# Windowed attention, a gated MLP and a channel mix: attention weights unfolded, values multiplied by whole and half key tiles

## The chip, the cores and the metric

The kernel runs on one core of a Trainium2 chip. The metric is the device time of one execution in microseconds (us). Three runs of the kernel before took 586.86 to 588.02 us, median 587.9. One further execution was profiled: 587.97 us by the same clock, with a span of 586.3 us from the first to the last traced instruction. The engines are PE (TensorE: matmuls; PEld is its weight load), DVE (VectorE), ACT (ScalarE), POOL (GpSimd) and SP, which issues all DMAs.

## The reference

Three layers follow each other; batch is 4, the sequence 576, the model width 512.

```python
# 1. attention: 8 heads of 64, a causal window of 128, ALiBi bias
scores = 0.125 * q @ k.T                                   # rel = query - key
scores = where((rel >= 0) & (rel < 128), scores - slope_h * |rel|, -1e9)
attn = exp(scores - max); attn /= sum(attn) + 1e-9
x = concat_heads(attn @ v)                                 # (4, 576, 512)
# 2. gated MLP with mixing over the sequence
h = gelu_tanh(x @ w_in); u, v = h[..., :512], h[..., 512:]
v_n = layernorm(v) * g_ln
v_s = w_sg @ v_n (over the sequence) + b_sg
x = x + (u * v_s) @ w_out
# 3. channel mix with a token shift
xk = mu_k*x + (1-mu_k)*x_prev; xr = mu_r*x + (1-mu_r)*x_prev
out = sigmoid(xr @ w_r) * (relu(xk @ w_k)**2 @ w_v)
```

Rows of the window matter below. Cut the sequence in 9 blocks of 64. A query block n sees key block n in its lower triangle, n-1 wholly, and n-2 in its strict upper triangle.

## The kernel before

**Recording and planning.** Helpers of `Build` record every operation with its cost in the author's model, with the engines that may do it (`"dp"`: DVE or POOL, `"ad"`: ACT or DVE, `"adp"`: all three) and with its reads and writes. `Rec.schedule` then picks an engine and an order for all of them by due times, shifted by the tables `PRI` and `ENG`. It also puts filler matmuls on `tri` (`filler`, names `wps`) where PE would idle. What comes out is one fixed order for each engine.

**Attention** works on 16 pairs of heads (two heads share the 128 partitions; four pairs make a batch). For each query block n of a pair, `s_item` makes scores of 64 queries against up to 192 keys on 64x64 quarters of the array, two heads at once. `s_tile` adds the mask and takes the maximum (DVE, L811), then exponentiates with row sums (ACT, L494). The exponentials p are 192 wide: key blocks n-2, n-1 and n. As n-2 holds a strict upper and n a lower triangle, L817 adds the one onto the other (the fold, `p<-p` 128x64), which leaves 128 columns. `t_step` and `t4_step` transpose these 9 blocks of a pair on PE (`tf<-ident,p`, 4, 4 and 1), copy them out of PSUM to `pf`, and split the fold again: `keep` makes an upper and a lower copy with a triangular select on POOL (L534) or a product with the mask `tri` on DVE (L541). `av_items` multiplies by the values (`a<-pf,rawv`): all 128 keys of a tile, two heads side by side on 128x64 halves of the array, 14 matmuls of 128 columns and 4 of 64. The first four pairs scale by the reciprocal row sum afterwards (`rt`, L879); the others scale p itself (L764). From pair 5 on (`MERGE`) the values' matmuls of pair c-1 and the first scores of pair c are one PE step (`av_s`).

**The MLP** of a batch (`moe1`) uses float32 split in a high and a low fp32r part (`xg`, `vhl`, `gg`, `w_in_t`, ...) and three products a group. `merge` interleaves the steps of batch b with the attention of batch b+1. Its PE groups are named `d`: `d<-w_in_t,xg` (v tiles, 512 columns), `d<-xg,w_in_t` (u tiles, 288), `d<-w_sg_t,vhl`, `d<-gg,w_out_t`. Weights arrive as 64-bit floats and are decoded on ACT and DVE (`wdec`) before the split.

**The channel mix** (`phase2`) runs last over chunks of 512 tokens: `d<-xk,wk`, then `rps<-w_r_t,xr`, then `vps<-w_v_t,k2h` and `k2l`.

**SBUF** is dealt out pool by pool in the order of `base`. With the sizes in the code, the pool `wp` begins at a multiple of 512 bytes. `xp` behind it has two buffers of 4x577 floats, each rounded up to 9,248 bytes, so that the tiles of the next pool `gp` (`xg`, `vhl`, `gg`, `k2h`, `k2l`) begin 64 bytes past a multiple of 512; `wk`, in another pool, begins 64 bytes short of one, and so do `xk`'s tiles.

Of the kernel before, what the change touches and what calls it, by code (L numbers as in the profile page):

```python
# [42 lines left out]
    ("rawv0", "sp"): -26306, ("rel", "pool"): 2432, ("rin", "dve"): 123164, ("rin.0", "dve"): 49476, ("rin.1", "dve"): 20510, ("rl", "act"): 67514,  # L43
# [4 lines left out]
    ("v.1", "dve"): -54577, ("v.1", "dve/pool"): 8029, ("vhl", "act/dve/pool"): -30835, ("vhl", "dve"): 107701, ("vhl", "dve/pool"): 115592,  # L48
    ("vhl.1", "act/dve/pool"): -138686, ("vhl.1", "dve"): -100786, ("vhl.1", "dve/pool"): 207877, ("vps", "pe"): -69329, ("vsg", "dve"): -48464,
    ("vsg", "dve/pool"): -215093, ("vsg.1", "dve"): 18451, ("vsg.1", "dve/pool"): 63786, ("w_in_t.0", "act/dve/pool"): 159389,  # L50
    ("w_in_t.0", "dve/pool"): -93050, ("w_out_t.1", "act/dve/pool"): -59118, ("w_out_t.1", "dve/pool"): -286676, ("w_r_t", "act/dve/pool"): -119201,
    ("w_r_t", "dve/pool"): 111587, ("w_sg_t.1", "act/dve/pool"): 278977, ("w_sg_t.1", "dve/pool"): -19852, ("w_v_t", "act/dve/pool"): -29476,
    ("w_v_t", "dve/pool"): 8489, ("wdec", "act"): 69975, ("wdec", "dve"): 110168, ("wdec.0", "act"): 285, ("wdec.0", "dve"): 657275,
# [562 lines left out]
def attn_gmlp_rwkv_kernel(  # L616
# [108 lines left out]
    def width(n):  # L725
        return 64 * min(n + 1, 3)
# [614 lines left out]
```

## Time and profile before

| | before |
|---|---|
| median of 3 runs | 587.9 us |
| the profiled execution | 587.97 us |
| its span | 586.3 us |
| PE busy | 573.0 us (98%) |
| DVE busy | 415.0 us (71%) |
| ACT busy | 289.7 us (49%) |
| POOL busy | 176.9 us (30%) |
| instructions | 11,019 |

Busy time counts an engine as occupied from the start of an instruction to its end; matmuls overlap each other, and fillers count as busy PE, so PE near 100% does not mean that all of it is wanted work. The 1.7 us between span and time lie around the traced instructions.

### The profile page before, as it was taken

Reading aid. Unit: us, or ns where it says so; the run is one execution under the profiler, and the core shown is the slowest. Engines: PE = TensorE matmul, PEld = TensorE weight load, DVE = VectorE, ACT = ScalarE, POOL = GpSimd, SP = SyncE. Lnnn points to the kernel's source line nnn. Section 1 sums busy time; section 2 is a strip of 40 time slices with the busy share of each in tenths; the row PEclk is TensorE's granted clock in tenths of the full one; section 3 lists DMA queues with packets and bytes.
Section 4 is the critical chain, followed back from the end, with each engine's and each line's share of the span. In section 5 each row is a group of like instructions: output and inputs, shape, how many; then the busy total and the mean of one; then the engine's idle time right before and its main releaser. Section 6 shows DMA issues by size and latency. Waiting matters only on the chain.

```text
span 586.3 us, 11019 instructions
## 1 busy us (share of the span) xinstructions
PE 573.0 (98%) x4050; PEld 486.0 (83%) x4050; DVE 415.0 (71%) x1174; ACT 289.7 (49%) x778; POOL 176.9 (30%) x321
## 2 busy tenths in 40 slices
PE   7898999999999999999999999999999999999997
PEld 4575789997899978999799987888888888888885
DVE  6999899876878768876899999962924463616032
ACT  4776787755665546762664377430503340413041
POOL 4534684753735527234355002300100000000000
PEclk9799999999999999999999999999999999999999
DMA  8765533324021220002713175331000100000000
GB/s 280 197 165 155 137 99 97 77 66 145 23 64 42 64 104 22 3 2 83 268 55 109 45 232 169 106 106 55 18 37 20 53 1 37 18 19 36 19 19 36
DMA packets 22998, 48.13 MB, mean 82 GB/s; under 512 B 4384, under 2 KB 12832, under 8 KB 22432
## 3 DMA queue, kind: packets, MB, share of 16 engines
q1 hardware_dynamic: 22944, 47.42, 26.6%
q8 instruction: 32, 0.52, 0.4%
q14 instruction: 22, 0.18, 0.1%
HBM read 37.97 MB, written 9.45 MB: 81 GB/s over the span
## 4 chain that ended last, share of the span: by engine, by line
PE 85%; DVE 10%; ACT 1%; issue 1%; POOL 1%; DMA 1%; SPq 0%; POOLq 0%; DVEq 0%; ACTq 0%
PE d L472 50%; PE vps L472 17%; PE rps L472 8%; PE s L472 4%; PE a L472 4%; PE tf L480 2%; DVE p L811 2%; DVE wdec L551 1%; DMA wraw<-in_w_sgT_dram 1%; DVE wdec L568 1%; DVE gt L551 1%; DVE p L514 0%; DVE v L551 0%; DVE w_sg_t L514 0%; DVE bn L998 0%
## 5 line engine op out<-in xcount | busy, mean ns | idle before, releaser
L472 PE MATMUL d<-xk,wk 128*128 128x512 f32 (+1 forms) x480 | 102.9, 368 | 0.0
L472 PEld LDWEIGHTS d<-xk,wk 128*128 128x128 f32 x480 | 84.4, 188 | 15.8
L472 PE MATMUL vps<-w_v_t,k2h 128*128 128x512 f32 x288 | 93.7, 396 | 0.0
L494 ACT ACTIVATE p<-p,nmax 128x192 f32<-128x192 f32 (+2 forms) x144 | 61.5, 429 | 30.0 <-DVE nmax L811 29.6
L472 PE MATMUL d<-w_in_t,xg 128*128 128x512 f32 (+1 forms) x240 | 63.1, 410 | 2.0 <-DVE xg L504 1.5
L472 PEld LDWEIGHTS vps<-w_v_t,k2h 128*128 128x128 f32 x288 | 54.1, 188 | 12.9
L472 PE MATMUL d<-w_sg_t,vhl 128*128 128x288 f32 x448 | 63.8, 298 | 0.0
L472 PEld LDWEIGHTS d<-w_sg_t,vhl 128*128 128x128 f32 x448 | 60.3, 188 | 1.7 <-issue 0.8
L472 PE MATMUL vps<-w_v_t,k2l 128*128 128x512 f32 x144 | 57.0, 396 | 0.0
L472 PEld LDWEIGHTS d<-w_in_t,xg 128*128 128x128 f32 (+1 forms) x240 | 42.3, 183 | 16.6 <-DVE xg L504 2.0
L472 PE MATMUL d<-xg,w_in_t 128*128 128x288 f32 x384 | 55.3, 299 | 0.3 <-ACT x L502 0.3
L472 PE MATMUL d<-gg,w_out_t 128*128 128x288 f32 x384 | 54.9, 297 | 0.0
L534 POOL TENSOR_SCALAR_AFFINE_SELECT pf<-pf 128x512 f32<-128x512 f32 (+2 forms) x70 | 43.4, 636 | 37.2 <-ACT pf L502 20.7
L472 PEld LDWEIGHTS d<-xg,w_in_t 128*128 128x128 f32 x384 | 52.0, 189 | 3.1 <-issue 1.1
L472 PE MATMUL rps<-w_r_t,xr 128*128 128x512 f32 x216 | 53.1, 392 | 0.3 <-ACT r L494 0.3
L472 PEld LDWEIGHTS d<-gg,w_out_t 128*128 128x128 f32 x384 | 51.9, 188 | 1.7 <-issue 1.4
L514 DVE TENSOR_TENSOR r<-vps,r 128x512 f32<-128x512 f32 x18 | 12.3, 687 | 54.5 <-ACT r L494 28.1
L472 PEld LDWEIGHTS rps<-w_r_t,xr 128*128 128x128 f32 x216 | 40.1, 188 | 9.2 <-ACT r L494 0.7
L811 DVE CUSTOM_DVE_ANT_0 p<-s,mask 128x192 f32<-128x192 f32 (+1 forms) x144 | 41.2, 328 | 8.1 <-PE s L472 8.1
L506 POOL TENSOR_SCALAR xk<-mt 128x64 fp32r<-128x64 f32 (+4 forms) x9 | 6.9, 766 | 130.6 <-DVE mt L551 129.3
L494 ACT ACTIVATE rl<-d 128x512 f32<-128x512 f32 (+1 forms) x40 | 21.7, 555 | 46.2 <-PE d L472 41.7
L494 ACT ACTIVATE r<-rps 128x512 f32<-128x512 f32 x18 | 10.7, 599 | 66.3 <-PE rps L472 66.2
(123 smaller groups left out, 996.0 us busy)
## 6 DMA issues: line engine op xcount, KB each, us to landing
rawqk<-in_qk_dram SPq DMA_DIRECT2D x32, 288.0 KB, 4.5
rawv<-in_v_dram SPq DMA_DIRECT2D x32, 160.0 KB, 2.3
xs<-x SPq DMA_DIRECT2D x4, 1154.0 KB, 4.7
out_dram<-r SPq DMA_DIRECT2D x18, 256.0 KB, 2.0
st<-in_w_in_dram SPq DMA_DIRECT2D x8, 512.0 KB, 7.3
wraw<-in_w_k_dram SPq DMA_DIRECT2D x8, 512.0 KB, 4.6
wraw<-in_w_v_dram SPq DMA_DIRECT2D x8, 512.0 KB, 3.7
wraw<-in_w_out_dram SPq DMA_DIRECT2D x8, 256.0 KB, 2.6
```

Source lines behind the costliest of these rows:

```text
L472: pe.matmul(real(o), real(l), real(r), start=st, stop=sp, **ex)
L480: pe.transpose(real(o), real(i), real(d))
L494: nc.scalar.activation(real(out), real(in_), func, scale=scale, **kw)
L506: alts.append(("pool", 148 + 0.83 * in_.n, lambda: nc.gpsimd.tensor_scalar(real(out), real(in_), 1.0, 0.0, ALU.mult, ALU.add)))
L514: alts.append(("dve", self._dve(out.n, False), lambda: nc.vector.tensor_tensor(real(out), real(a), real(b), op)))
L534: nc.gpsimd.affine_select(out=real(out), in_=real(in_), pattern=pat, compare_op=cmp, fill=0.0, base=0, channel_multiplier=-sgn)
L551: alts.append(("dve", cost or self._dve(out.n, False, isinstance(s, Vw)), lambda: nc.vector.scalar_tensor_tensor(real(out), real(a), real( ...
L568: alts.append(("dve", self._dve(out.n, fast and not a.ps, ptr), lambda: nc.vector.tensor_scalar(real(out), real(a), real(s1), real(s2), op ...
L811: K.raw("dve", 70 + w / 0.96, lambda: nc.vector.tensor_tensor_reduce(out=real(po), in0=real(s), in1=real(ma), scale=-0.125, scalar=3.0e38, ...
```

## The change

1. For the first 8 pairs (`UNF`), p is neither folded nor masked. Two neighbouring query blocks share a tile p of 384 columns, and `t_step` transposes 13 blocks of 128x128 (4, 4, 4, 1) where there were 9. The later pairs fold, transpose 9 and mask as before, with one select for each kind of triangle.
2. For all pairs, `av_items` multiplies each whole key tile t with the two query blocks that see all of it (2t+1, 2t+2) on 128x64 halves, and the half tiles with the one query block each that sees 64 of its keys, on 64x64 quarters. The upper halves of a tile go to a second PSUM tile `e`, which is added to x afterwards: one more DVE operation a pair, two in the first four pairs.
3. `tri` has 20 blocks and is made by 6 selects on POOL and 2 copies on DVE.
4. In `base`, `xp` goes behind `gp` and `up`, so that `xg`, `vhl`, `gg`, `k2h` and `k2l` begin at multiples of 512 bytes.
5. The cost of float32 matmuls in the planner's model is new, and `PRI` and `ENG` have other numbers throughout.

```diff
-    ("a", "pe"): -69879, ("a.0", "pe"): 271509, ("a.1", "pe"): 145744, ("bn", "dve"): -21776, ...
+    ("a", "pe"): 374006, ("a.0", "pe"): 37152, ("a.1", "pe"): -13497, ("bn", "dve"): 212851, ...
...
+UNF = 8
+KEEP = ((0, 0), (1, 1), (0, 0), (1, 1), (0, 0), (0, 1), (1, 0), (0, 1), (1, 0), (0, 1))
...
-          "attc": 1, "raw": 3, "wraw": 2, "v": 4, "sp": 20, "pt": 2,
+          "attc": 1, "raw": 3, "wraw": 2, "v": 4, "sp": 10, "pt": 2,
-    base = ("const", "wp", "xp", "gp", "up", "tp", "st", "dr", "psD", "psS", "psT")
+    base = ("const", "wp", "gp", "up", "xp", "tp", "st", "dr", "psD", "psS", "psT")
...
     def s_tile(c, n, bank):
-        p = T("sp", [P, 192], F32, "p")
+        if n % 2 == 0:
+            PP[c] = T("sp", [P, 384], F32, "p")
+        p = PP[c]
...
+        f = po
+        if c >= UNF:
+            f = 320 if n % 2 else 0
+            if n > 1:
+                K.tt(p[:, f:f + 64], p[:, o:o + 64], p[:, o + 128:o + 192], ALU.add, "dp")
+            k = 128 if n == 0 else o + 64 * (n % 2)
+            f = p[:, k:k + 128]
+            PW[c].append(f)
+        elif n % 2 or n == 8:
+            PW[c] += [p[:, k:k + P] for k in ((128, 256) if n == 1 else (0, 128) if n == 8 else (0, 128, 256))]
+        PT[c, n] = f
+
+    def t_steps(c):
+        return ((0, 4), (4, 8), (8, 9)) if c >= UNF else ((0, 4), (4, 8), (8, 12), (12, 13))
...
+        if c >= UNF:
+            z = max(b, 2)
+            K.keep(pf[:, 14 + 2 * z:14 + 2 * e, :], pf[:, 2 * z:2 * e, :], 0)
+            K.keep(v, v, 6 if b else 4)
...
         for t in range(4):
             for j in range(2):
-                its.append((a[64 * j:64 * j + 64, 2 * t:2 * t + 2, :], rv[j][:, t, :], pair(4 * t, j), t == 0, t == 3, SG))
-            if t < 3:
-                for j in range(2):
-                    its.append((a[64 * j:64 * j + 64, 2 * t + 2:2 * t + 4, :], rv[j][:, t, :], pair(18 + 4 * t, j), False, False, SG))
-        for k, i in ((3, 30), (4, 16)):
+                r, w = slice(64 * j, 64 * j + 64), (6 if un else 4) * t + 3 - j
+                if t < 3:
+                    its.append((a[r, 2 * t + 1:2 * t + 3, :], rv[j][:, t, :], pf[:, w:w + 2 + 2 * j:1 + 2 * j, :], t == 0, False, SG))
+                else:
+                    its.append((a[r, 7, :], rv[j][:, t, :], pf[:, w, :], False, False, SG))
+                    its.append((e[r, 0, :], rv[j][:, t, :], pf[:, w + 1 + 2 * j, :], True, False, SG))
+        for j in range(2):
+            r = slice(64 * j, 64 * j + 64)
+            its.append((e[r, 0, :], rv[j][:, 4, :], pf[:, (24 if un else 30) + j, :], False, False, SG))
+        for i in range(4):
+            lo, up = (6 * i, 6 * i) if un else (14 + 4 * i if i else 0, 16 + 4 * i)
             for j in range(2):
-                its.append((a4b[64 * j:64 * j + 64], rv[j][:, k, :], pf[:, i + j, :], k == 3, k == 4, SG))
-        return a, a4b, its
+                its.append((a[64 * j:64 * j + 64, 2 * i, :], rv[j][0:64, i, :], pf[0:64, lo + j, :], False, i == 3, SG))
+            for j in range(2):
+                if i:
+                    its.append((e[64 * j:64 * j + 64, i, :], rv[j][64:P, i - 1, :], pf[64:P, up + 1 - j, :], False, i == 3, SG))
+        return a, e, its
...
+        x = x_t[b]
+        xo, odd = x[:, ch, 129:513].split(P)[:, :, 64:P], e[:, 1:4, :]
         if c < RROW:
-            K.tt(x_t[b][:, ch, 1:513], a.flat(), rt, ALU.mult)
+            K.tt(x[:, ch, 1:513], a.flat(), rt, ALU.mult)
+            ro = rt[:, 128:512].split(P)[:, :, 64:P]
+            K.tt(ro, odd, ro, ALU.mult)
+            odd = ro
         else:
-            K.copy(x_t[b][:, ch, 1:513], a.flat())
-        K.copy(x_t[b][:, ch, 513:577], a4b)
+            K.copy(x[:, ch, 1:513], a.flat())
+        K.tt(xo, xo, odd, ALU.add, "dp" if c < RROW else "d")
+        K.copy(x[:, ch, 513:577], e[:, 0, :])
...
+    for x in sorted(set(KEEP)):
+        for k in (k for k in range(len(KEEP)) if KEEP[k] == x and k not in (2, 3, 8, 9)):
+            v = K.tri[:, 2 * k:2 * k + 2].two()
+            K.raw("pool", 240, lambda v=v, f=K.select(v, *x): f(real(v), real(v)), [v], [v])
+    for k in (2, 8):
+        K.copy(K.tri[:, 2 * k:2 * k + 4].flat(), K.tri[:, 2 * k - 4:2 * k].flat(), "d")
```

On PE, the values' matmuls of pair 1 before (`a` and the numbered `a` are its two PSUM tiles, the second for the last query block), with the scores and transposes behind them:

```order
L472 MATMUL a<-pf,rawv 64x128 x14
L472 MATMUL a_585<-pf,rawv 64x64 x4
L472 MATMUL s<-rawqk 64x192 x2
L480 MATMUL tf<-ident,p 128x128 x8
L472 MATMUL s<-rawqk 64x64 x2
```

The same place after (`a_540` is the tile `e` of the code):

```order
L488 MATMUL a<-pf,rawv 64x128 x6
L488 MATMUL a<-pf,rawv 64x64
L488 MATMUL a_540<-pf,rawv 64x64
L488 MATMUL a<-pf,rawv 64x64
L488 MATMUL a_540<-pf,rawv 64x64 x3
L488 MATMUL a<-pf,rawv 64x64 x4
L488 MATMUL a_540<-pf,rawv 64x64 x2
L488 MATMUL a<-pf,rawv 64x64 x2
L488 MATMUL a_540<-pf,rawv 64x64 x2
L488 MATMUL a<-pf,rawv 64x64 x2
L488 MATMUL a_540<-pf,rawv 64x64 x2
L488 MATMUL s<-rawqk 64x192 x2
```

Fourteen wide matmuls have become six; the last 14 narrow ones are the quarters, `a` from the lower 64 keys and `a_540` from the upper 64.

On DVE, between the masked scores of pairs 1 and 2, before (`st_405` is staged `w_in`):

```order
L514 TENSOR_TENSOR p<-p 128x64
L504 COPY pf<-tf_530 128x128
L514 TENSOR_TENSOR p<-p 128x64
L541 TENSOR_TENSOR pf<-pf,tri 128x128
L568 TENSOR_SCALAR wdec<-wdec 128x512
L541 TENSOR_TENSOR pf<-pf,tri 128x128
L514 TENSOR_TENSOR p<-p 128x64 x2
L551 SCALAR_TENSOR_TENSOR wdec<-st_405,wdec 128x512
```

The same place after:

```order
L596 TENSOR_SCALAR wdec<-wdec 128x512
L579 SCALAR_TENSOR_TENSOR wdec<-st_408,wdec 128x512
L520 COPY rt<-rt 128x512
L596 TENSOR_SCALAR wdec<-wdec 128x512
L530 TENSOR_TENSOR w_in_t<-wdec,w_in_t 128x512
L530 TENSOR_TENSOR x<-a,rt 128x512
...
L530 TENSOR_TENSOR rt<-a_540,rt 128x3x64
L579 SCALAR_TENSOR_TENSOR wdec<-st_408,wdec 128x512
L530 TENSOR_TENSOR x<-x,rt 128x3x64
```

Folds and mask products are gone from the row; the two operations on the second PSUM tile have come in.

On POOL, from the making of `tri` on, before:

```order
L1199 MEMSET tri 128x1024
L877 MEMSET x 128x4
L534 AFFINE_SELECT tri<-tri 128x512 x2
L516 TENSOR_TENSOR p<-p 128x64 x3
L534 AFFINE_SELECT pf<-pf 128x512
L820 MEMSET p 128x64
L571 TENSOR_SCALAR p<-p,rin 128x128
```

After:

```order
L1245 MEMSET tri 128x1280
L546 AFFINE_SELECT tri<-tri 128x128 x6
L848 MEMSET p 128x64 x2
L522 TENSOR_SCALAR w_in_t<-wdec 128x512
L848 MEMSET p 128x64 x2
L522 TENSOR_SCALAR w_in_t<-wdec 128x512
```

POOL has lost folds and selects here and takes part of the split of `w_in`.

## Rows read from the trace of the kernel before

**Rows 1.** The page: an engine's busy time; the granted clock in 40 slices, tenths.

```profile
PE 573.0 (98%) x4050; PEld 486.0 (83%) x4050; DVE 415.0 (71%) x1174; ACT 289.7 (49%) x778; POOL 176.9 (30%) x321
...
PEclk9799999999999999999999999999999999999999
```

**Rows 2.** Stretches of the span: their length, each engine's busy time (instructions), clock, DMA.

```profile
10.00:92.00 82.00, 75.92 (x806) 57.35 (x804) 76.62 (x278) 62.47 (x206) 42.88 (x83) 0.94 0.60 161
92.00:280.00 188.00, 188.00 (x1723) 171.17 (x1724) 146.46 (x465) 110.94 (x344) 93.75 (x170) 1.00 0.21 62
280.00:360.00 80.00, 79.98 (x477) 71.75 (x475) 75.70 (x147) 47.66 (x87) 24.27 (x34) 1.00 0.44 149
360.00:587.00 227.00, 222.19 (x1008) 182.70 (x1008) 111.01 (x268) 65.68 (x135) 10.58 (x14) 1.00 0.12 40
```

**Rows 3.** PE in order of time: start, length, instructions merged [idle time before, its releaser].

```profile
22.82 0.33 PE L472 MATMUL s<-rawqk 64*64 64x64 f32 x4 [1.66 <-ACT x L502]
...
56.45 0.50 PE L472 MATMUL d<-w_in_t,xg 128*128 128x512 f32 x1 [1.46 <-DVE xg L504]
```

**Rows 4.** The chain of waits from 0 to 110 us: start, length, what it passes through.

```profile
17.39 0.44 DVE pf L541
...
19.04 0.67 DVE w_in_t L514
19.71 0.41 DVE p L514 x3
...
23.87 1.33 PE s L472 x12
...
40.70 0.36 DVE p L811
...
54.42 0.74 DVE w_sg_t L514 x2
...
90.77 0.78 DVE p L568 x4
```

**Rows 5.** DVE and POOL groups up to 92 us: count, busy time, mean ns, idle before.

```profile
L514 DVE TENSOR_TENSOR p<-p 128x64 f32<-128x64 f32 x30 | 7.1, 255 | 0.7 <-ACT p L494 0.7
L541 DVE TENSOR_TENSOR pf<-pf,tri 128x128 f32<-128x128 f32 x7 | 2.7, 383 | 0.0
...
L534 POOL TENSOR_SCALAR_AFFINE_SELECT pf<-pf 128x512 f32<-128x512 f32 x18 | 13.9, 779 | 6.0 <-DVE pf L541 3.8 <-ACT pf L502 1.7
L516 POOL TENSOR_TENSOR p<-p 128x64 f32<-128x64 f32 x19 | 7.6, 409 | 6.8 <-ACT p L494 6.4
```

**Rows 6.** PE in order of time: values, then scores; the x12 are its end.

```profile
153.13 1.98 PE L472 MATMUL a<-pf,rawv 128*64 128x128 f32 x36
...
154.49 0.62 PE L472 MATMUL a<-pf,rawv 128*64 128x128 f32 x12
155.04 0.77 PE L472 MATMUL s<-rawqk 64*64 64x64 f32 x16
```

**Rows 7.** PE in batch 1's v tiles, in order of time.

```profile
138.41 7.26 PE L472 MATMUL d<-w_in_t,xg 128*128 128x512 f32 x30
145.51 1.04 PE L480 MATMUL tf<-ident,p 128*128 128x128 f32 x8
146.31 1.65 PE L472 MATMUL d<-w_in_t,xg 128*128 128x512 f32 x6
```

**Rows 8.** The chain of waits from 340 us on.

```profile
371.59 6.82 PE d L472 x30
...
394.94 14.01 PE vps L472 x60
...
425.68 2.75 PE rps L472 x12
```

**Rows 9.** The start, in order of time: POOL's `tri`, DVE's first masked score.

```profile
5.18 1.35 POOL L534 TENSOR_SCALAR_AFFINE_SELECT tri<-tri 128x512 bf16<-128x512 bf16 x2
...
7.41 0.23 DVE L811 CUSTOM_DVE_ANT_0 p<-s,mask 128x64 f32<-128x64 f32 x1 [0.61 <-PE s L472]
```

More of the change, by code (lines that the diff above doesn't have):

```diff
@@ L48 @@
[L48 to L51, printed above, removed]
@@ new lines @@
+    ("rawv0", "sp"): -136893, ("rel", "pool"): 41476, ("rin", "dve"): 34972, ("rin.0", "dve"): -509504, ("rin.1", "dve"): 1422,
[3 rows of a table added]
+    ("tri", "dve"): -22967, ("tri", "pool"): 133552, ("u", "dve"): -55884, ("u.1", "dve"): 217151, ("v", "dve"): -90958, ("v", "dve/pool"): 707269,
+    ("v.1", "dve"): -119475, ("v.1", "dve/pool"): 106315, ("vhl", "act/dve/pool"): 56077, ("vhl", "dve"): -212679, ("vhl", "dve/pool"): -383927,
+    ("vhl.1", "act/dve/pool"): 53485, ("vhl.1", "dve"): 21972, ("vhl.1", "dve/pool"): -79968, ("vps", "pe"): 142878, ("vsg", "dve"): 40,
@@ L175, in real @@
                 a = a.bitcast(x)
+            elif k == "sp":
+                a = a.rearrange("p (a b) -> p a b", b=x)
+            elif k == "two":
+                a = a.rearrange("p (s h) q -> p s h q", h=2)
             elif k == "bro":
@@ L461, in mm @@
     def mm(self, items, **kw):
-        cost = 0.0
-        for o, l, r, *_ in items:
-            cost += 14.0 if o.box()[0] >= 64 and o.ids.shape[0] <= 64 or l.ids.shape[0] == 64 <= l.box()[0] else (4 * r.n / 2.4 + 10) if l.dtype == F32 else (r.n / (1.2 if l.dtype == BF16 else 2.4) + (20 if l.base.name in ("k2h", "k2l") else 14))
-        if items[0][1].dtype == F32 and (items[0][1].ids.shape[0] == 64 or items[0][1].ids.shape[1] == 64):
-            cost += 320.0
+        tiled = [(i[1].ids.shape[0] <= 64, i[1].ids.shape[1] <= 64) for i in items]
+        if items[0][1].dtype == F32 and any(map(any, tiled)):
+            free, t = {}, 0.0
+            for (o, l, r, *_), (rt, ct) in zip(items, tiled):
+                at = [(a, c) for a in ((l.box()[0] // 64,) if rt else (0, 1)) for c in ((o.box()[0] // 64,) if ct else (0, 1))]
+                t = max([t] + [free.get(x, 0.0) for x in at])
+                for x in at:
+                    free[x] = t + 4 * r.n / 2.4
+            cost = max(free.values()) + 255 + 215 * sum(x != y for x, y in zip(tiled, tiled[1:]))
+        else:
+            cost = sum(r.n / (1.2 if l.dtype == BF16 else 2.4) + 14.0 for _, l, r, *_ in items)
         pe = self.nc.tensor
@@ L524, in square, with select, go, keep @@
             ("pool", 140 + 2.12 * x.n, lambda: nc.gpsimd.tensor_tensor(real(x), real(x), real(x), ALU.mult))], [x, x], [x])
-    def keep(self, out, in_, upper, engs="p"):
-        nc = self.nc
-        m = in_.ids.shape[1]
-        sgn, cmp = (-1, ALU.is_gt) if upper else (1, ALU.is_ge)
-        pat = [[0, m // 4], [64 * sgn, 2], [0, 2], [sgn, 64]] if m % 4 == 0 else [[0, 2], [sgn, 64]]
+    def select(self, v, upper, odd):
+        sgn, cmp = (-1, ALU.is_gt) if upper else (1, ALU.is_ge)
+        def go(out, in_):
+            self.nc.gpsimd.affine_select(out=out, in_=in_, pattern=[[0, v.ids.shape[1]], [0, 2], [sgn, 64]],
+                                         compare_op=cmp, fill=0.0, base=64 * sgn * odd, channel_multiplier=-sgn)
+        return go
+    def keep(self, out, in_, k0, engs="dp"):
+        nc = self.nc
+        m = in_.ids.shape[1] // 2
+        kinds = KEEP[k0:k0 + m]
+        parts = []
+        for x in sorted(set(kinds)):
+            ks = [k for k in range(m) if kinds[k] == x]
+            vo, vi = (z.two()[:, ks[0]:ks[-1] + 1:2 if len(ks) > 1 else 1] for z in (out, in_))
+            parts.append((self.select(vo, *x), vo, vi))
+        t = self.tri[:, 2 * k0:2 * (k0 + m), :]
         def go():
-            nc.gpsimd.affine_select(out=real(out), in_=real(in_), pattern=pat,
-                                    compare_op=cmp, fill=0.0, base=0, channel_multiplier=-sgn)
+            for f, vo, vi in parts:
+                f(real(vo), real(vi))
         alts = []
-        if "p" in engs and not in_.ps:
-            alts.append(("pool", 147 + 0.715 * out.n, go))
-        t = self.tri[:, int(upper), :m, :]
+        if "p" in engs:
+            alts.append(("pool", 147 * len(parts) + 0.715 * out.n, go, len(parts)))
         if "d" in engs:
             alts.append(("dve", self._dve(out.n, False), lambda: nc.vector.tensor_tensor(real(out), real(in_), real(t), ALU.mult)))
-        return self.r.op(alts, [in_] + ([t] if "d" in engs else []), [out])
+        return self.r.op(alts, [in_, t], [out])
     def sub(self, out, a, hi, engs="dp"):
@@ L847, in av_items @@
         a = T("psD", [P, 8, 64], F32, "d", "a") if c >= NC else T("psT", [P, 8, 64], F32, "t", "a")
-        a4b = T(pool, [P, 2, 256], F32, "s" if pool == "psS" else "t", "a4")[:, 0, 0:64]
+        e = T(pool, [P, 2, 256], F32, "s" if pool == "psS" else "t", "a4").flat()[:, 0:256].split(64)
         pf, its = PTc.pop(c), []
         rv = [rawv.pop(2 * c + j) for j in range(2)]
-        def pair(i, j):
-            lo, hi = i + j, i + 3 - j
-            return pf[:, min(lo, hi):max(lo, hi) + 1:abs(hi - lo), :]
+        un = c < UNF
@@ L914, in trans @@
         def trans():
-            for b in range(2):
-                add(480, t_step, prev, b)
-            add(120, t4_step, prev)
+            for b, e in t_steps(prev):
+                add(120 * (e - b), t_step, prev, b, e)
         def tail():
```

152 lines of the change are left out of this document (71 added, 81 removed), and 43 rows, old and new, of the table PRI.

## The prediction

> **What bounds the kernel now.** I read the busy times first: PE 98%, DVE 71%, ACT 49%, POOL 30% [rows 1]. That says PE, but busy PE includes fillers, so the stretches come next [rows 2]. From 92 us to the end PE is busy without a break, and DVE has room in most of it (146.5 of 188 us from 92 to 280); only from 280 to 360 is DVE nearly full too (75.7 of 80). Before 92 us it is the other way round: DVE is busy 76.6 of 82 us, and PE waits for x and its split ("ACT x", "DVE xg") [rows 3]. The chain of waits agrees: it runs over DVE's short operations from about 7 to 24 us, over PE from 23.87 to 40.70, and over DVE again from there to 92 [rows 4]. So there are two stages with two prices. Up to 92 us (the front) an instruction is worth what it takes DVE, about 68 of those 85 us. After that only PE's time counts.
>
> **The front: DVE's list.** I counted the two orders up to the first `vsg`, which is the first result of batch 0's third product; both versions have by then done the values of pairs 0 to 5, so the lists compare. DVE issues 311 instructions before and 272 after.
>
> Gone are 30 folds: three in a row take 0.41 us on the chain, 0.137 each [rows 4], 4.1 us. (Their busy time, 7.1 us for the 30 [rows 5], counts overlap with the neighbours, so I take steps along the chain throughout.) Gone are 10 mask products, 7 of 128 columns and 3 of 256; the one shown took 0.44 us on the chain and the 7 were busy 2.7 us, 0.38 each [rows 4, 5]; at 0.30 to 0.40 each, 3.4 us. 11 scalings of p at 0.78/4 = 0.195 make 2.1 [rows 4]. Seven splits of `w_sg` go to POOL at 0.74/2 = 0.37 [rows 4], 2.6. Ten copies and scalings of 288 to 576 columns go to POOL or ACT; I put them at the price of such a split, some 0.4 each, 4.0. Sum 16.2.
>
> New are four splits of `vhl` and one of `xg`, at 0.67 at most like that of `w_in_t` [rows 4], 3.1; four casts of `w_in_t`, a third product's width at under that price, say 0.35, 1.4; ten operations of 128x192 on the second PSUM tile, whose form is not in the trace: between the fold's 0.137 (64 columns) and 0.37 (288), by width 0.27, 2.7 (bounds 1.4 to 3.7); three scalings of 192 columns, 0.25 each, 0.8; two copies of `tri`, 0.2 to 0.5 each, 0.6; five others, 1.5. Sum 10.1. Net 6.1 us less on DVE, with 4.5 to 7.5 as bounds from those of the parts.
>
> Does another engine take over? POOL loses 24 selects of the two kinds and 19 folds, over 21 us of its 43 [rows 2, 5], and gets seven splits and some casts: no. ACT gets 16 scalings of 192 columns for 14 of 128, six copies out of PSUM (13 transposed blocks a pair, not 9) and loses six casts of `w_in_t`: about 3.5 us on 62.5 of 82 [rows 2]. It stays under DVE's share, but not by much. PE gets four more transposes a pair and has fillers to give up. So of the 6.1 us, the share that lies on DVE's part of the chain is gained: 68/85, 4.9 us.
>
> At the very start something is lost. The first masked score on DVE starts at 7.41 us, 0.9 us after POOL's selects of `tri`, which take 1.35 us [rows 9]. Now six selects on POOL make `tri`, and two copies on DVE, which wait for the selects, stand in DVE's queue ahead of the first masked score; everything on DVE waits behind them. At 0.3 us each the selects end about 0.7 us later, the copies add 0.6, and the 0.9 us in between absorb most: 0.3 us lost (0 to 1.2). Front: -4.6 us (range 0 to -8; below nothing too if PE's clock, 0.94 over the front and 7 tenths in the second slice [rows 1, 2], is granted in full).
>
> **After 92 us: the values on PE.** In units of 128 columns and one of float32's two passes, a pair takes 16 units before (14 wide matmuls are 7 side by side, 2 passes each; 4 narrow ones make 2). The x36 rows start at 153.13 and the last x12 at 154.49: 12 units in 1.36 us, 0.113 each; the remaining 4 units take 0.45 of the 0.55 us up to the scores, which leaves 0.10 for the change from halves to quarters [rows 6]. After: three wide pairs 6 units, the narrow ones on halves 3, the quarters 4 rounds of 64 columns, 4 units if all four quarters work at once. 13 units: 3 x 0.113 = 0.34 us less. The new change from halves to quarters costs 0.10, but where scores follow in the same step (they are on quarters already) the old one goes. Behind the front lie pairs 6 to 15: nine with scores behind, 9 x 0.34, and the last one 0.24, together 3.3 us. Against that stand four more transposes for pairs 6 and 7: 0.80/8 = 0.10 each from 145.51 to 146.31 [rows 7] and a copy group more, 1.1 us. Net -2.2 us (0 to -3.3).
>
> The Trainium skill (TensorEngine Tiling (Array Packing), Key Properties) has it that a change of tiling mode drains TensorE; the 0.10 us above is in line with that, and a rule of a much dearer drain is not seen here. The same page (Gotcha 1, PSUM Pressure) says that row tiles can't use one PSUM bank at the same time; the lower halves write `a` and the upper `e`, in two banks, so by the rule the quarters still overlap; if they did not, the first rival below would hold.
>
> **After 92 us: the place of the activations.** The chain prices 512-column matmuls by their stationary tile: `k2h`/`k2l` (64 bytes past 512) 14.01/60 = 233.5 ns, `xr` (on a multiple) 2.75/12 = 229.2, `wk` (64 short of one) 6.82/30 = 227.3 [rows 8]; `xg`, also 64 past, 7.10/30 = 236.7 [rows 7]. So being off a multiple alone does not cost; being 64 past goes with 4 to 6 ns more. Put on a multiple, I take them to `xr`'s 229.2: 4.3 ns for 432 matmuls of `vps` and 180 of the v tiles behind the front, 2.6 us. Bounds: nothing (it was something else about these groups), or 6.2 ns, 3.8 us. The 288-column groups all have one `gp` operand and I have no clean one to compare, so I take nothing; 4.3 ns for their 1,120 would be 4.8 more.
>
> **Elsewhere nothing.** In 92 to 280 us DVE gets work that POOL had and the x additions: by the two orders 15 splits of `gg` more at 0.37, six of `vhl` and seven of `xg` at 0.67, ten additions at 0.27, less some casts, so some 15 us; it has 41 idle [rows 2]. Were that cover gone, it would cost what is then late. From 280 to 360 us the lists are alike.
>
> Sum: -4.6 - 2.2 - 2.6 = -9.4 us against the profiled 587.97 (586.3 of span and 1.7 around it; the median is 587.9): 578.6 us.
>
> **Rivals.** *The quarters do not overlap by rows.* Then they take 7 rounds, not 4: 3 units, 0.34 us a pair, 3.4 us behind the front. For it: no row shows quarters with new weights every 64 columns. Against: the scores do overlap on quarters. 582.0 us.
>
> *ACT takes over the front.* Its load rises to 66 of what would be 77 us, and it now empties PSUM more often; the front gains 1 us instead of 4.6. 582.2 us.
>
> *The 512 bytes do nothing.* `wk` is off a multiple too and fastest. 581.2 us.
>
> *The second PSUM tile holds PE up: slower.* `e` has more readers than the tile before it: DVE's addition, only on DVE from pair 4 on, and the copy of the last block. `psT` and `psS` have two buffers each, and transposes or scores wait for the one that `e` holds. The trace has such a wait once, 1.66 us for ACT's copy into x [rows 3]. Against: behind the front PE never waited. Were it paid by each of the ten pairs there, 16.6 us: 595.2. It decides from about six pairs (9.4/1.66).
>
> **How the numbers follow.** Forecast 0.50, quarters 0.10, ACT 0.14, bytes 0.14, second tile 0.12. The two runs' spread is 0.1 to 0.2%, so under 0.2% (1.2 us) is no change. The first four cases are all faster, except where two or three of them meet (0.03, about 587 us). Some of the last case costs little: 0.05 stay within faster. Faster 0.88, the same 0.05, slower 0.07. Range: the parts' far ends do not all meet; below, the front at -8, the values at -3.3 and the bytes at -3.8 give 572.9; above, two rivals together 585. I take 572 to 586.
>
> **What would show it.** The first `d<-w_sg_t,vhl` 4 to 5 us earlier than before, with DVE still near full ahead of it; a step of values at 1.5 to 1.6 us where scores follow, not 1.9; `vps` at 229 ns; no idle PE from there to 360 us. It is wrong if the front ends at the same time, if `vps` stays at 233, or if PE waits for x's additions.

## The result

The changed kernel takes 572.93 us (median of 4 runs, 572.48 to 573.70), the kernel before 587.38 (4 runs on the same chip): ratio 0.976, 95% interval 0.9735 to 0.9784. That is 14.5 us where 9.4 were forecast; 578.6 us was the forecast and 572 to 586 its range. The profiled execution took 573.35 us, its span is 571.6. In a later set it was timed again, on the chip of that set: 573.07 us against 584.75, ratio 0.9793 (0.9768 to 0.9819).

The span has one milestone in both versions, the first matmul of `d<-w_sg_t,vhl` on PE, in the prediction the end of the front. By groups, the line after it (count, least, median and most ns, first and last start):

```profile
L488 PE MATMUL d<-w_sg_t,vhl x448: 288/294/402, 83.6 to 308.8; 128*128 128x288 f32 x150
```

Before, it starts at 93.8 us. So the front became 10.2 us shorter (4.6 were forecast) and all behind it 4.5 (4.8 were forecast: 2.2 for the values, 2.6 for the 512 bytes). The question is the front. The stretch up to there, of the kernel before and then of the changed one (length; busy time and instructions of PE, PEld, DVE, ACT, POOL; clock, DMA share, GB/s):

```profile
0.00:93.80 93.80, 84.63 (x858) 62.22 (x859) 83.65 (x302) 67.25 (x219) 49.07 (x104) 0.95 0.61 165
```

```profile
0.00:83.60 83.60, 75.78 (x959) 57.48 (x960) 72.18 (x261) 68.44 (x225) 31.64 (x82) 0.98 0.68 188
83.60:570.00 486.40, 483.87 (x3363) 422.15 (x3362) 338.99 (x904) 218.70 (x553) 121.71 (x215) 1.00 0.21 67
```

DVE is busy 11.5 us less, not 6.1, POOL 17.4 us less, ACT 1.2 more. The page answers to [rows 1]: PE's clock now has its low slice at the very start only.

```profile
PE 559.7 (98%) x4320; PEld 479.6 (84%) x4320; DVE 411.2 (72%) x1164; ACT 287.1 (50%) x776; POOL 153.4 (27%) x297
...
PEclk8999999999999999999999999999999999999999
```

The chain of waits after, from 24 to 84 us, answers to [rows 4] (start, length, what it passes through). ACT has come onto it in two places, and from 56.90 us on it is PE's, but for 1.9 us of DVE at 68.52. Before, 38.5 of the 51.3 us from 40.70 to 92 were DVE's (the pieces of that chain, summed by engine).

```profile
24.98 1.17 DVE w_in_t L530 x2
...
26.55 1.86 ACT p L510 x8
...
49.01 2.37 ACT p L606 x7
...
51.87 0.95 ACT pf L518 x2
...
56.15 0.70 DVE v L579
56.90 3.01 PE d L488 x12
...
68.52 0.69 DVE pf L520
...
69.81 0.60 DVE v L579
```

Behind the front, a step of values with scores behind it starts at 88.42 and its first score at 90.08 us; in [rows 6] that took 1.91 us, here 1.66 (PE in order of time: start, length, instructions merged):

```profile
88.42 1.88 PE L488 MATMUL a<-pf,rawv 128*64 128x128 f32 x51
90.08 0.27 PE L488 MATMUL s<-rawqk 64*64 64x128 f32 x1
90.08 0.22 PE L488 MATMUL a<-pf,rawv 64*64 64x64 f32 x1
90.09 0.76 PE L488 MATMUL s<-rawqk 64*64 64x64 f32 x15
90.78 2.12 PE L488 MATMUL d<-w_sg_t,vhl 128*128 128x288 f32 x14
```

And 60 matmuls of `vps` took 14.01 us on the chain in [rows 8], 233.5 ns each; after, 13.60, which is 226.7:

```profile
383.80 2.76 PE rps L488 x12
386.56 13.60 PE vps L488 x60
```

### The profile page after: what moved, and what is told of

The parts are those of the page before. It is cut to its first block, busy times and chain, and to the rows that moved or that the text cites. A ratio compares the mean times of both kernels' runs of the same rounds, so it can differ in the third digit from the quotient of the medians.

```text
span 571.6 us, 11531 instructions
## 1 busy us (share of the span) xinstructions
PE 559.7 (98%) x4320; PEld 479.6 (84%) x4320; DVE 411.2 (72%) x1164; ACT 287.1 (50%) x776; POOL 153.4 (27%) x297
## 4 chain that ended last, share of the span: by engine, by line
PE 91%; DVE 5%; POOL 1%; ACT 1%; issue 1%; POOLq 0%; ACTq 0%; DVEq 0%
PE d L488 54%; PE vps L488 17%; PE rps L488 9%; PE a L488 4%; PE s L488 4%; PE tf L496 3%; DVE p L842 1%; DVE wdec L579 1%; DVE w_in_t L530 1%; DVE mask L596 0%; ACT p L606 0%; POOL pf L546 0%; DVE x L530 0%; PE rt L488 0%; DVE pf L520 0%
## 5 line engine op out<-in xcount | busy, mean ns | idle before, releaser
L488 PE MATMUL vps<-w_v_t,k2h 128*128 128x512 f32 x288 | 95.3, 391 | 0.0
L488 PEld LDWEIGHTS vps<-w_v_t,k2h 128*128 128x128 f32 x288 | 54.0, 188 | 11.5
L488 PE MATMUL d<-w_in_t,xg 128*128 128x512 f32 (+1 forms) x240 | 60.9, 400 | 0.9 <-DVE xg L530 0.6
L518 ACT CAST k2h<-rl 128x512 fp32r<-128x512 f32 (+1 forms) x20 | 11.4, 586 | 81.2 <-PE vps L488 80.5
L488 PEld LDWEIGHTS d<-w_in_t,xg 128*128 128x128 f32 (+1 forms) x240 | 40.8, 177 | 13.2 <-issue 1.4
L488 PE MATMUL rps<-w_r_t,xr 128*128 128x512 f32 x216 | 50.6, 390 | 0.0
L522 POOL TENSOR_SCALAR k2h<-rl 128x512 fp32r<-128x512 f32 (+1 forms) x14 | 8.9, 640 | 124.6 <-PE vps L488 122.1
L488 PE MATMUL s<-rawqk 64*64 64x192 f32 (+2 forms) x576 | 34.0, 320 | 1.9 <-DMA rawqk<-in_qk_dram 1.3
L510 ACT ACTIVATE gt<-d 128x288 f32<-128x288 f32 (+2 forms) x52 | 24.6, 476 | 14.9 <-PE d L488 11.4
```

Source lines behind the costliest of these rows:

```text
L488: pe.matmul(real(o), real(l), real(r), start=st, stop=sp, **ex)
L510: nc.scalar.activation(real(out), real(in_), func, scale=scale, **kw)
L518: alts.append(("act", self._act(in_), lambda: nc.scalar.copy(real(out), real(in_))))
L522: alts.append(("pool", 148 + 0.83 * in_.n, lambda: nc.gpsimd.tensor_scalar(real(out), real(in_), 1.0, 0.0, ALU.mult, ALU.add)))
```

## The experiments

Four theories for the front: (1) DVE's list got shorter; (2) POOL's selects and folds slowed DVE, and most are gone; (3) PE's clock was halved for a while in the profiled execution of before, and isn't after; (4) the new tables alone make a better order. All runs in one table (us; "values" is the start of the first values' matmuls on PE; the front ends at the first `d<-w_sg_t,vhl`; "rest" is span less front; these three are of the one profiled execution; ratios to the kernel before on the same chip, with 95% intervals):

| run | values | front | rest | median | ratio |
|---|---|---|---|---|---|
| before | 18.1 | 93.8 | 492.5 | 587.38 | 1 |
| after | 16.8 | 83.6 | 488.0 | 572.93 | 0.976 (0.9735-0.9784) |
| e12_after_again | 15.5 | 82.6 | 488.0 | 573.07 | 0.9793 (0.9768-0.9819) |
| e1_place | 18.4 | 91.5 | 489.3 | 582.43 | 0.9962 (0.994-0.9983) |
| e2_oldplace | 18.3 | 85.4 | 490.8 | 576.59 | 0.9854 (0.9829-0.9879) |
| e3_fold_all | 17.8 | 102.5 | 487.2 | 591.24 | 1.0106 (1.0081-1.0132) |
| e4_oldtables | 16.9 | 95.5 | 493.4 | 594.95 | 1.015 (1.0112-1.0188) |
| e5_dve_back | 18.4 | 88.1 | 488.2 | 577.59 | 0.9849 (0.9823-0.9875) |
| e6_pool_back | 16.8 | 91.3 | 488.4 | 580.30 | 0.9906 (0.9882-0.993) |
| e10_pool_memset | 17.0 | 89.2 | 488.1 | 578.90 | 0.9884 (0.9861-0.9907) |
| e7_clock | 18.3 | 91.6 | 492.5 | 584.76 | 0.9976 (0.9959-0.9993) |
| e8_rows_apart | 18.4 | 93.9 | 491.4 | 585.56 | 1.0002 (0.9982-1.0022) |
| e9_rows_apart2 | 18.3 | 85.3 | 489.4 | 575.05 | 0.9828 (0.9803-0.9854) |
| e11_unf6 | 17.0 | 84.8 | 492.0 | 577.99 | 0.9874 (0.9853-0.9896) |

The rest is worth a look first. Four kernels with what the changed one does behind the front, and fronts from 82.6 to 91.3 us (e5, e6, e10, e12), have a rest of 488.0 to 488.4. So the front passes on to the end one for one, and the two stages can be priced apart, as the prediction did.

The front itself must be read with care. after, e12, e2 and e9 have one order up to the milestone (only the quarters differ in e9), and end the front at 82.6 to 85.4 us. From the first values on they all take 66.9 to 67.1 us: the difference is made ahead of them, in what is called the start below, where the same matmuls on PE can take longer. The first 16 score matmuls of 192 columns and the first values, in e12 and then in e2:

```profile
7.62 1.15 PE L488 MATMUL s<-rawqk 64*64 64x192 f32 x16 [0.58 <-DVE nmax L842]
...
15.52 1.84 PE L488 MATMUL a<-pf,rawv 128*64 128x128 f32 x52
```

```profile
8.02 1.82 PE L488 MATMUL s<-rawqk 64*64 64x192 f32 x16 [0.44 <-DVE nmax L842]
...
18.30 1.84 PE L488 MATMUL a<-pf,rawv 128*64 128x128 f32 x52
```

The granted clock reads 1.00 from 0 to 20 us in both, so the cause stays open. Where two starts differ, fronts are therefore compared from the first values on. Nor is the profiled execution always near the run's median: that of e4 took 590.63 us, where the median is 594.95.

**The place of the activations: e1_place and e2_oldplace.** The edit of e1, to the kernel before; e2 is the reverse, to the kernel after.

```diff
-    base = ("const", "wp", "xp", "gp", "up", "tp", "st", "dr", "psD", "psS", "psT")
+    base = ("const", "wp", "gp", "up", "xp", "tp", "st", "dr", "psD", "psS", "psT")
```

> The kernel before with one edit: the pool that holds the split activations (gp) is opened after the weights instead of after the x tiles, so that its tiles start on a multiple of 512 bytes and not 64 past one. No instruction moves. If the place prices the 512-column matmuls (forecast): vps falls from 233.5 to 228.5 ns a matmul, the v tiles likewise, the first third product of batch 0 (d<-w_sg_t,vhl) still starts at 93.8 us, and the time is 587.4 - 2.6 = 584.8 us (ratio 0.9956). If the place does nothing and something else in the change made vps shorter: vps 233.5 ns and 587.4 us (ratio 1.000 within 0.001).

> The kernel after with the pools opened in the old order, so that gp stands 64 bytes past a multiple of 512 again. If the place is the price: vps back at 233.5 ns, the front ends at 83.6 us as in the kernel after, time 572.9 + 2.6 = 575.5 us (against before 0.9798). If the place does nothing: 572.9 us (0.9754).

The rest falls by 3.2 us from before to e1 and rises by 2.8 from after to e2; forecast 2.6. The chain of the old kernel in the new place, then of the new one in the old place:

```profile
391.92 13.64 PE vps L472 x60
```

```profile
389.01 14.00 PE vps L488 x60
```

227.3 and 233.3 ns each: `vps` follows the place and nothing else. (The fronts were expected where before and after have them; e1's came 2.3 us earlier, for which the clock is the likely reason, see e7, and e2's 1.8 us later, which is its start.) The rest not due to the place is 1.7 (before to e2) or 1.3 us (e1 to after).

**Half of the change: e3_fold_all and e4_oldtables.** In the first `UNF = 0` (the second PSUM tile and its operations on DVE stay), in the second the block of numbers is that of the kernel before; the first one's edit:

```diff
-UNF = 8
+UNF = 0
```

> The kernel after with no pair left unfolded: all sixteen pairs are folded and masked and take 9 transposes, as before; the values on quarters, the tables of the order and the place of the activations stay those of the kernel after. Theory 1 (the front's gain of 10.2 us is DVE's list, made shorter by the folds and mask products): the front ends near 93 us again, DVE is busy about 83 us up to there, and the time is 572.9 + 10.2 - 1.1 (8 transposes fewer on PE behind the front) = 582 us, ratio 0.991. Rival (the new tables alone order the front better, or the half clock of PE between 24 and 31 us was what cost): the front ends at 85 to 88 us and the time is 573 to 577 us, ratio 0.976 to 0.982.

> The kernel after with the tables of the order (PRI, ENG and the other numbers of that block) of the kernel before. Theory 1 (what is computed in the front decides): the front ends at 84 to 87 us, since the tables were made for another list, and the time is 573 to 577 us (ratio 0.976 to 0.982). Rival (the tables are the gain): the front ends near 93 us and the time is about 583 us (ratio 0.992).

Both expectations missed: each half alone is slower than before. The stretch up to the front's end in e3, then in e4, and in e4 what PE waited for from 10 to 96 us (total, times, longest):

```profile
0.00:102.50 102.50, 86.47 (x982) 63.81 (x983) 89.98 (x329) 71.41 (x232) 52.18 (x122) 0.92 0.59 161
```

```profile
0.00:95.50 95.50, 80.70 (x980) 60.75 (x981) 79.42 (x276) 67.25 (x216) 26.33 (x67) 0.96 0.62 169
```

```profile
PE tf L499 <- ACT p L609: 6.2, 4, 3.0
PE tf L499 <- DVE x L533: 1.8, 1, 1.8
```

Folded pairs under the new tables put 329 instructions on DVE ahead of the milestone (before 302); unfolded ones under the old tables have 276 (after 261), and PE waits for p on ACT. Theory 4 falls, and theory 1 as it was put falls with it: list and order give the gain together, and it can't be shared out between them (undone singly, they cost 18.9 and 11.9 us of front, more than the 10.2 in all).

**DVE's price: e5_dve_back.** Order and all else as after, but for one fill of the scratch on POOL.

```diff
...
+        if 1 < n and c < 5:
+            EXTRA[id(R.ops[-1])] = [lambda: nc.vector.tensor_tensor(
+                real(relb[:, 256:320]), real(relb[:, 320:384]), real(relb[:, 384:448]), ALU.add)]
...
```

> The kernel after with 35 additions of 128x64 more on DVE, on scratch that nothing else reads, one behind each masked score (from the third of a pair on) of pairs 0 to 4; nothing else moves. A fold of this size takes 215 ns alone in the trace of before (22 of the 30 folds of the front had no POOL work beside them). Theory 1 (DVE's own time sets the front): DVE busy up to the front's end goes from 72.2 to about 79 us, the front ends at 83.6 + 4.8 (35 x 0.137) to 83.6 + 7.5 (35 x 0.215), 88.4 to 91 us, and the time is 578 to 580 us (ratio 0.984 to 0.987). Rival (DVE has room in the front now, 72 of 83.6 us): at most 1 us later, 574 us (ratio 0.977).

The front ends 4.5 us later and the median is 4.7 above after's, just under what theory 1 expected; the rival's 1 us is out. 4.7/35 is 0.134 us for each addition, but the start is in it: the first values came at 18.39 us here, and 11 of the additions lie ahead of them. From there on the front takes 69.7 us instead of 66.9 to 67.1, which is 0.11 to 0.12 us for each of the other 24. Both are near the step of 0.137 on the chain in [rows 4], and not the length of 218 ns. So DVE still sets most of the front, and the price of a fold with no POOL work beside it was about right in the sum. The added group up to 88.1 us (busy time, mean ns, idle before):

```profile
L848 DVE TENSOR_TENSOR rel<-rel 128x64 f32<-128x64 f32 x35 | 7.6, 218 | 0.0
```

**POOL beside DVE: e6_pool_back and e10_pool_memset.** e6 puts selects and folds on POOL, into scratch; e10 has fills of about the same time, each behind a one-column copy that waits for the same data. Of the edits, the first line below is in both; then `-` is what e6 calls there and `+` what e10 has in its place.

```diff
...
+            EXTRA[id(o)] = [lambda: sel(v.flat(), 0), lambda: sel(v.flat(), 1)]
...
             def sel(x, k):
-                y = relb[:, 256 + 512 * k:768 + 512 * k]
-                nc.gpsimd.affine_select(out=real(y), in_=real(x), pattern=[[1, 512]], compare_op=ALU.is_ge, fill=0.0, ...)
+                nc.gpsimd.tensor_scalar(real(relb[:, 1400 + k:1401 + k]), real(x[:, 0:1]), 1.0, 0.0, ALU.mult, ALU.add)
+                nc.gpsimd.memset(real(relb[:, 256:736]), 0.0)
...
```

> The kernel after with POOL's work of the kernel before put back on it as results that nothing reads: two selects of 128x512 for each full group of transposed blocks and one 128x64 addition behind four of the nine scores, pairs 0 to 4; DVE, ACT and PE run what they run in the kernel after. Theory 2 (POOL's selects and folds made DVE's copies and folds slower: beside POOL's work a fold took 388 ns, alone 215, a 128x512 subtraction 934 and 683, in the trace of before): DVE busy up to the front's end rises from 72.2 to 75 or more though its list is the same, and the front ends 2 to 4 us later, 575 to 577 us (ratio 0.980 to 0.984). Theory 1 alone (DVE's list is all): DVE stays at 72 us, the front at 83.6 us, 573 us (ratio 0.976).

> As the run with POOL's old work put back, with the same waits and about the same time on POOL, but with fills of scratch in place of the selects and folds, so that POOL reads next to nothing (each with a one-column copy ahead that waits as the select or fold did). Theory 2 (POOL's reads make DVE slower): DVE busy up to the front's end stays near 73 us, a 128x192 addition at 350 ns and not 473, and the front ends at 84 to 87 us, ratio 0.977 to 0.981. Rival (POOL's queue: its own splits and scalings come late behind the added work): DVE near 73 us too, but the front ends at 89 to 91 us, ratio 0.988 to 0.991.

DVE's work is the same in both and in the kernel after. Groups of DVE up to the front's end, and that stretch, in e6 and then in e10:

```profile
L530 DVE TENSOR_TENSOR x<-x,rt 128x192 f32<-128x192 f32 x4 | 2.6, 662 | 0.0
L530 DVE TENSOR_TENSOR rt<-a,rt 128x192 f32<-128x192 f32 x4 | 1.4, 351 | 0.0
```

```profile
0.00:91.30 91.30, 79.53 (x958) 60.00 (x959) 78.80 (x261) 68.95 (x224) 62.34 (x132) 0.96 0.61 172
```

```profile
L530 DVE TENSOR_TENSOR x<-x,rt 128x192 f32<-128x192 f32 x4 | 1.4, 350 | 0.0
L530 DVE TENSOR_TENSOR rt<-a,rt 128x192 f32<-128x192 f32 x4 | 1.4, 349 | 0.0
```

```profile
0.00:89.20 89.20, 79.43 (x959) 59.31 (x960) 73.71 (x261) 69.28 (x225) 60.76 (x182) 0.94 0.64 176
```

An operation with two operands in SBUF takes 662 ns beside POOL's selects and folds and 350 beside its fills; the one with an operand in PSUM (`a`) takes 350 in both. DVE's busy time goes from 72.2 to 78.8 with the selects and only to 73.7 with the fills, at nearly the same load on POOL. So theory 2 is shown as far as DVE's time goes. The kernel before has it too: three folds with no POOL work beside them, and two in a select (DVE and POOL in order of time):

```profile
19.64 0.48 DVE L514 TENSOR_TENSOR p<-p 128x64 f32<-128x64 f32 x3
...
49.18 1.79 POOL L534 TENSOR_SCALAR_AFFINE_SELECT pf<-pf 128x512 f32<-128x512 f32 x2 [1.52 <-ACT pf L502]
...
50.33 0.84 DVE L514 TENSOR_TENSOR p<-p 128x64 f32<-128x64 f32 x2
```

The Trainium skill (SBUF — State Buffer, SBUF: two separate sides) has it that the two engines share a pair of SBUF ports as an exclusive lock, and that a DVE operation with two SBUF inputs meets it only against POOL work that reads SBUF; the 662, 350 and 351 ns agree.

For the end, though, the rival expectation of e10 came out: with fills that leave DVE nearly alone the front still ends 5.6 us later, for POOL's queue is now in the way. In e6 it ends 7.7 us later, where theory 2 expected 2 to 4. PE's waits in e10 from 10 to 90 us, where the kernel after has 0.7 in the first row, and what the clock did behind that wait (stretches; the clock is the third number from the end):

```profile
PE tf L496 <- POOL p L599: 2.6, 1, 2.6
```

```profile
34.00:36.00 2.00, 0.08 (x1) 0.09 (x1) 1.65 (x6) 0.91 (x5) 1.86 (x3) 0.86 0.32 75
36.00:38.00 2.00, 2.00 (x18) 1.08 (x18) 0.09 (x1) 1.57 (x4) 0.91 (x4) 0.50 0.00 0
38.00:40.00 2.00, 2.00 (x35) 1.79 (x36) 1.97 (x10) 1.69 (x9) 1.08 (x5) 0.50 0.00 0
```

In e6 that wait was 2.9 us, one of 2.4 us for ACT's p came beside it, and the clock fell there too (0.58 from 27 to 31 us, 0.50 from 42 to 44). e6 and e10 differ by 2.1 us of front, and their intervals overlap. What the slower DVE cost at the end is therefore not settled by them.

**The clock: e7_clock.** Before, with 20 fillers where PE waits ahead of [rows 3]'s first row.

```diff
...
+            if o.pe and o.lab == "tf.0" and seen[0] == 1:
+                seen[1] += 1
+                if seen[1] == 1:
+                    for _ in range(NHOLE):
+                        fl.eng[2]()
...
```

> The kernel before with 20 filler matmuls more on PE, put into the stretch at about 21 to 24 us in which PE has nothing to do; the result is the same. In the profile of before PE's clock is 0.66 in the slice 20 to 30 us, in that of the first experiment (same instructions) 0.83. Theory 3 (part of the front's gain is the clock that PE was granted there): the slice is granted 0.95 or more, the front ends at 90 to 91 us and the time is 0.5 to 3 us under that of before, the more the lower the clock of before's own runs (ratio 0.995 to 0.999). Rival (the clock there costs nothing since DVE is what ends last): the front stays at 91.5 to 93.8 us, or grows by what the fillers take, ratio 1.000 to 1.003.

Stretches of the kernel before, then of e7:

```profile
22.00:24.00 2.00, 0.47 (x8) 0.33 (x12) 2.00 (x6) 1.40 (x5) 0.61 (x2) 0.78 0.90 225
24.00:27.00 3.00, 3.00 (x21) 2.15 (x22) 3.00 (x12) 2.35 (x6) 2.11 (x4) 0.50 0.93 225
27.00:31.00 4.00, 4.00 (x26) 2.38 (x24) 2.16 (x12) 3.87 (x17) 2.10 (x5) 0.63 1.05 255
```

```profile
20.00:24.00 4.00, 3.84 (x46) 2.94 (x44) 4.00 (x12) 2.41 (x6) 0.56 (x2) 1.00 0.62 156
24.00:31.00 7.00, 6.87 (x80) 4.76 (x80) 6.76 (x31) 6.89 (x25) 4.45 (x8) 1.00 0.96 227
```

Before, PE all but stands from 21 to 24 us and then runs at half clock, 1.2 GHz, up to about 30; with the fillers it stays at 2.4. The front ends at 91.6 instead of 93.8 us with the start nearly the same (18.1 and 18.3) and the rest at 492.5 in both, so some 2.2 us of the profiled front was clock. Clock and time are as theory 3 expected; the end of the front is in the rival's range and not in its own 90 to 91. e1 agrees: it has the instructions of before, without fillers, its clock was low for half as long (0.54 from 24 to 27 us, 0.92 from 27 to 31), and its front ends at 91.5. Over the runs the fillers gain 1.0 us of median. The runs show the clock too: of 23 of the kernel before in that set, the eight with a mean clock of 0.988 to 0.991 took 586.8 to 588.1 us and the fifteen at 0.996 or 0.997 took 583.7 to 585.8; the twelve of e7, all at 0.994 or more, 583.4 to 585.8. The profiled execution of before had 0.991. That is probably also why the ratio of the changed kernel is 0.976 in one set and 0.979 in the other: three of the four runs of before took 586.9 us or more in the first set, and three of eleven took 586.8 or more in the second.

**The quarters: e8_rows_apart and e9_rows_apart2.** The upper rows' quarters follow the lower ones; in e8 as recorded and so planned anew, in e9 only as PE issues them.

```diff
-        for i in range(4):
+        for h, i in [(0, 0), (0, 1), (0, 2), (0, 3), (1, 1), (1, 2), (1, 3)]:
...
```

> The kernel after with the values' quarters in another order: first all that stand on the array's lower rows, then all on the upper rows, so that two row halves are no longer side by side; same instructions. If quarters overlap by rows (forecast): the quarters take 7 rounds and not 4, the step of values grows from 1.67 to 2.0 us, 0.34 us for each of ten pairs behind the front, time 576.3 us (ratio 0.982). If they don't overlap anyway (first rival of the prediction): the step stays at 1.67 us and the time at 572.9 us (ratio 0.976).

> The values' quarters again first all on the lower rows and then all on the upper, as in the eighth run, but now only where PE issues them: every other instruction on every engine stands as in the kernel after. In the eighth run a step of values with scores behind it took 2.53 us from its first matmul to the end of the scores against 2.36 in the kernel after, and all matmuls of values 29.7 us against 27.0, but its front was 10 us longer too. If those 10 us came from the order that was planned anew: the front ends at 84 to 86 us, the time is that of the kernel after plus 2 to 3 us (ratio 0.980). If the quarters' rows themselves cost the front: it ends near 94 us, ratio 1.000.

In e8 I had overlooked that the planner would order everything anew: its front ended 10.3 us later, and its time says nothing about quarters. e9 says more. It is 2.0 us above e12 on the same chip, with intervals that overlap, and its later front is the start. But its rest is 1.4 us longer, and a step of values with scores behind, to the next product, takes 92.66 - 90.13 = 2.53 us where the kernel after takes 90.78 - 88.42 = 2.36 (PE in order of time; the other eight such steps behind the front differ by 0.17 too):

```profile
90.13 1.89 PE L490 MATMUL a<-pf,rawv 128*64 128x128 f32 x46
...
92.03 0.71 PE L490 MATMUL s<-rawqk 64*64 64x128 f32 x12
92.66 2.11 PE L490 MATMUL d<-w_sg_t,vhl 128*128 128x288 f32 x14
```

So quarters on different rows do overlap, and apart they cost 0.17 us a step (forecast 0.34; the rows show the last ones now beside the scores).

**A better version: e11_unf6, with e12_after_again beside it.**

```diff
-UNF = 8
+UNF = 6
```

> The kernel after with six pairs unfolded and not eight. Pairs 6 and 7 come where PE has no more idle time (from 57 us on), so each of their 4 extra transposes costs 0.1 us on PE, and DVE has room for their folds and masks. The order on DVE is that of the kernel after up to its 224th row, close to the front's end. By theory 1: 0.8 us less than the kernel after, 572.1 us (ratio to it 0.9986). Rival (DVE's extra work near 75 us delays PE, or the changed order does): 573 to 577 us.

> The kernel after once more, on the chip of this set, to compare the three above with it: ratio 0.976 to before, front 83 to 85.5 us.

e11 is 4.9 us slower than e12, not 0.8 faster: 4.0 us in the rest and 2.2 in the front, of which 1.4 are the start. What PE waited for from 84 to 170 us in e11; e12 has no such wait from 82 to 170. Then DVE in order of time ahead of the first of them:

```profile
PE d L488 <- DVE vsg L579: 1.2, 1, 1.2
PE a L488 <- DVE vsg L579: 1.2, 1, 1.2
PE d L488 <- ACT x L518: 0.8, 1, 0.8
```

```profile
87.27 0.69 DVE L569 TENSOR_TENSOR pf<-pf,tri 128x512 f32<-128x512 f32 x1
...
88.20 0.89 DVE L569 TENSOR_TENSOR pf<-pf,tri 128x512 f32<-128x512 f32 x2
89.01 0.45 DVE L579 SCALAR_TENSOR_TENSOR gt<-gt,d 128x288 f32<-128x288 f32 x1
89.37 0.51 DVE L579 SCALAR_TENSOR_TENSOR vsg<-d,gln,bsg 128x288 f32<-128x288 f32 x1
```

The masks of the folded pairs stand in DVE's queue ahead of `vsg`, which empties the PSUM tile that PE needs next. Room in DVE's busy share was no cover. None of the versions tried beats the changed kernel.

## Why the prediction was too small

**The step that failed** is "Net 6.1 us less on DVE, with 4.5 to 7.5 as bounds". DVE is busy 11.5 us less up to the milestone. The count of instructions was about right (39 fewer by the orders, 41 in the traces); what it left out is that the operations which stay get shorter when POOL's selects and folds go. Where POOL works beside a DVE instruction, take its length less the median of its shape without POOL beside it, from the fronts of before, after, e6 and e10 together: over the front that sums to 6.4 us before (161 instructions), 2.5 after (91), 8.4 in e6 and 3.8 in e10. Of the 11.5 us some 3.9 are then this, an estimate from few undisturbed readings (2.9 if only shapes with three or more of them count), and 7.6 the list, at the far bound. The prediction had the 24 selects and 19 folds in the sum, but only as time that POOL gets back. A hint stood in [rows 5]: a fold's mean length is 255 ns there, and 215 for those without POOL work beside them.

**The share that turns DVE's time into the front's was misread too.** "68/85" counts all of the chain outside 23.87 to 40.70 us as DVE's. Summed by engine from 7 to 92 us, the chain has 49.1 us of DVE, 24.5 of PE, 3.9 of DMA, 3.1 of ACT and 4.3 that waited for nothing shown: 0.58 for DVE and not 0.80. The two errors work against each other: 6.1 x 0.80 is 4.9, and 11.5 x 0.58 is 6.7. That the front's term is not further off is luck.

**Two parts of the 10.2 us are not the change's gain.** The clock of the profiled execution of before is 2.2 us, by e7; the prediction had it as a bound ("if PE's clock is granted in full"), not as a term. The start is 1.4 us (first values at 18.1 us before, 16.8 after), and the changed order itself had them between 15.5 and 18.3. Without both, from the first values on, the front takes 73.3 us in e7 and 66.9 to 67.1 in the four kernels with the changed order: 6.2 to 6.5 us gained, near the 6.7 above. The whole came out at 572.93 us, 0.9 inside the range's lower end, with a front beyond its own range of 0 to -8; that it stayed inside is luck as well. (The chances, as worked out, come to 0.90 for faster and 0.03 for the same, not 0.88 and 0.05.)

**Behind the front the sum held**: 4.8 forecast, 4.5 measured. The 512 bytes gave 2.8 to 3.2 (forecast 2.6). Values and transposes gave 1.3 to 1.7 (forecast 2.2): a step with scores behind it gained 0.25 us and not 0.34, in eight of nine (0.28 in the other). The 0.10 for a change of halves to quarters, dropped there since an old one went, may still be paid; but the last pair, charged with it, gained 0.10 us to the next product and not 0.24, so the quarters cost more than was taken for them in another way too. That was not tested.

**The rivals.** Quarters overlap by rows (e9). ACT did not take over, but came nearer: busy 68.4 of 83.6 us, and on the chain for 7.4 us where it had 3.1 before (15.7 in e12). The bytes do count (e1, e2). The second PSUM tile holds nothing up behind the front: the one idle stretch of PE over 0.1 us from there to 360 us is 0.4 us at 219.74, for POOL's `v`. And DVE's first masked score lost nothing: it came at 6.83 us, where [rows 9] have 7.41.

**What stays open**: how the 6.2 to 6.5 us divide between a shorter list, an undisturbed DVE and an order that fits both, since e3 and e4 don't add up and e10 moved the wait to POOL; and why the start takes longer in some executions.

## What to carry to other kernels

Work that is taken off POOL can shorten DVE's operations too: price it also by the DVE operations with two SBUF operands that run beside it, from rows with and without POOL work next to them. Sum a chain of waits by engine before a share is read from it. Before two fronts of single executions are compared, look whether they started alike. Where a planner orders the work, an experiment that changes its input tests the new order and not the edit; change what is issued in a fixed order instead. Room in an engine's busy share covers added work only if nothing that another engine waits for stands behind it in its queue.

## What the runs showed of the hardware

Beside POOL work that reads SBUF, DVE's 128x192 addition of two SBUF operands took 662 ns instead of 350; with one operand in PSUM, or beside fills, it kept its 350. A 512-column matmul of `vps` took 226.7 to 227.3 ns with its stationary operand on a multiple of 512 bytes and 233.3 to 233.5 with it 64 bytes past one, in both kernels. After waits of 1.7 and 0.7 us close together (before) and of 2.6 us (e10), PE was granted half its clock, 1.2 GHz, for some 7 us, while it was busy without a break; twenty fillers in the first gap kept it in full. The first 16 score matmuls of 192 columns took 1.82 us in one execution and 1.15 in another, at a granted clock of 1.00 in both.
